# A decode kernel: the last weight matrix laid out in blocks of 14 and 13, a part of it in a transfer of 64 rows

## The chip, the cores and the metric

The kernel runs on one core of one Trainium2 chip. The metric is the device time of one execution, in microseconds; the kernel before has a median of 712.53 us over three runs (712.04 to 712.59). A core has the engines TensorE (PE in the profile, with its weight loads as PEld), VectorE (DVE), ScalarE (ACT), GpSimd (POOL) and SyncE (SP), and sixteen DMA engines that move data from the chip's memory into the on-chip store. SP does no arithmetic here: it only issues the loads.

## The reference

Two rounds of the same two layers on a batch of four tokens, with the same weights and the same caches in both rounds:

```python
x = A_x                                              # 4 x 1 x 640
for _ in range(2):
    x = x + A(layernorm(x), k_cache, v_cache, wq, wo)   # attention
    x = x + B(layernorm(x), w1, w2)                     # MLP

# A: 32 heads of 128, the last 1024 of 4096 cached keys
q = x @ wq ; s = einsum("bhqd,bhkd->bhqk", q, k) * 128 ** -0.5
o = einsum("bhqk,bhkd->bhqd", softmax(s), v) ; return o @ wo
# B: 640 -> 1728 -> 640
return maximum(x @ w1, 0) @ w2
```

All arrays are 32-bit floats. The weights and caches don't fit on the chip together, so nearly all of them are read twice, some 300 MB in all, for very little arithmetic per byte.

## The kernel before, in words

The 128 partitions (rows) of the on-chip store hold the data; `store` is one large tile of five slots and a first part, `ring` and `kept` are small ones. The host lays all of a head's data (wq, keys, values, wo) out as one record of 9472 columns on 128 partitions; heads go through the slots one after another. `rec` is the tensor of the records and `wm` that of w1 and w2.

*The order of the loads.* The Python code first builds a list, `items`, of all loads in their order. `pump()` issues from its front on SP whenever `done(...)` has freed the columns that the next load will overwrite; it never reorders. Loads share eight completion semaphores in turn, and a load waits until the one eight places ahead of it has landed. So SP runs ahead of the data by at most eight loads.

*The order on the engines.* `InOrder` (the helper in which nearly every instruction is recorded, so that most profile rows carry its line, L102) issues the instructions of each engine in the order in which the code calls them.

*Round two's MLP*, `mlp(1)`, stands at the end of the program. The transposed, normalised x is in `xT`; `h_ps` is a PSUM bank. For each of five blocks of w1, four matmuls write h for a quarter j of the 1728 features, 432 columns wide, on partitions 32j to 32j+3. VectorE then transposes h in blocks of 32 x 32 into `hT` (a view of `scratch`), and takes the maximum with zero times the layer norm's factor. So features lie in `hT` as block m of each quarter on 32 partitions: thirteen full blocks of 32 and one of 16, since 432 is 13 times 32 and 16 more. w2 is stored to match: `TILES` lists 52 pieces of 128 partitions x 160 columns (block m, output quarter n) and, as entries 28 and 29, two more that pack the half blocks of 16 features (`ENDS`); each of these two is used by two matmuls. The DVE copy of 16 columns ahead of the second transpose lets the two halves of those packed pieces meet the right features.

*Loads of w2 in round two.* They come last of all, in four loads of 22, 20, 8 and 4 pieces (`W2_SLOT`), into the slot that head 23's record had; w1 goes to the slot beside it, in three loads. The heads 24, 25 and 26 are the last three of the round. `query`, `scores`, `values` and `project` are what a head does on TensorE, in this order; `project`, with wo at the end of a record, is the last.

*Fillers.* `busy()` is a matmul of no use to the result, on 328 columns unless another width is given, into spare columns of `acc`. They stand where TensorE would wait. A matmul of 32-bit floats is recorded as two passes, each with a weight load, so a filler counts as two in the profile.

After the last w2 matmul VectorE copies `acc` to `x_sb` (in `scratch`) and SP stores it as `out`.

Of the kernel before, what the change touches and what calls it, by code (L numbers as in the profile page):

```python
# [38 lines left out]
P = 128  # L39
B, D, H, DH, W, FF = 4, 640, 32, 128, 1024, 1728  # L40
NB = 4
FD = D // NB
# [10 lines left out]
FQ = FF // NB  # L53

TILES = [(m, n) for m in range(13) for n in range(NB)]
ENDS = 28
TILES[ENDS:ENDS] = [(13, 0), (13, 1)]
TCOLS = len(TILES) * FD
RING = 4320
KEPT = WO - 4 * 512  # L60
FIRST = K + 3 * 512
# [2 lines left out]
W2 = KB * FF  # L64
WM = W2 + TCOLS


W2_RING = [8, 5, 16, 10, 11, 4]
# [6 lines left out]

CUTS = [*range(0, K, DH), *range(K, WO, 512), *range(WO, REC + 1, FD)]
W1_SLOT = [[0, 1], [2, 3], [4]]
W2_SLOT = [22, 20, 8, 4]
LATE = 6


# [25 lines left out]


@with_exitstack
def decode_kernel(ctx: ExitStack, tc: tile.TileContext, xf, rec, wm, out):  # L110
    nc = tc.nc
    pe, dve, act, pool, sp = (InOrder(tc, e) for e in (nc.tensor, nc.vector, nc.scalar, nc.gpsimd, nc.sync))
    sb = ctx.enter_context(tc.tile_pool(name="sb", bufs=1))
# [10 lines left out]
    hT = scratch.rearrange("p (m j) -> p m j", j=32)  # L124
# [4 lines left out]
    rows = sb.tile([P, 2 * B], F32, name="rows")  # L129
# [6 lines left out]
    store = sb.tile([P, FIRST + NS * REC], F32, name="store")  # L136
    kept = sb.tile([P, REC - KEPT], F32, name="kept")
    ring = sb.tile([P, RING], F32, name="ring")

# [3 lines left out]
    acc = ps.tile([P, 512], F32, name="acc")  # L143
# [30 lines left out]
    LAST = H - NS  # L174


    def home(h, r):

        if r:
            return FIRST + (h if h >= LAST else h - 6 + LAST) % NS * REC  # L180
        return (0 if h < NS else FIRST) + h % NS * REC

    items = []
# [3 lines left out]
    spare = home(H - 1, 0)  # L187
    buffers = {"store": store, "ring": ring, "kept": kept}

    def load(src, lo, hi, buf, col, parts):  # L190
        items.append((src[:, lo:hi], buf, col, hi - lo, parts))

    def place(buf, col):
        return ("store", spare + FROM + col) if buf == "spare" else (buf, col)

    def weight(r, lo, hi, buf, col):
        buf, col = place(buf, col)
        load(wm, lo, hi, buf, col, [(("w", r), lo, hi, col)])


    def run(r, lo, hi, buf, col):
        parts = [(("rec", r, h), max(lo - h * REC, 0), min(hi - h * REC, REC), col + max(h * REC - lo, 0))
                 for h in range(lo // REC, (hi - 1) // REC + 1)]
        load(rec, lo, hi, buf, col, parts)
# [44 lines left out]
    for lo, hi, buf, col in IN_RING:  # L249
# [3 lines left out]
        (0, V, 0, WO), (2, 0, 2, V), (1, V, 1, REC), (3, 0, 3, V), (2, V, 2, REC), (3, V, 4, FROM))]  # L253
    places += [("store", 0, FIRST), ("store", old[4] + FROM, old[4] + REC), ("ring", 0, RING)]
    cuts = [h * REC + x for h in new[1:6] for x in CUTS]
    c, end = new[1] * REC, new[6] * REC
    for buf, lo, hi in places:
        if lo == old[1]:
            piece(1, new[0], WO, REC, buf, lo)
        elif c < end:  # L260
            cut = max(x for x in cuts if x <= min(end, c + hi - lo))
            run(1, c, cut, buf, lo)
            c = cut
# [6 lines left out]
    ending(1, hs, False)  # L270
    for ks in W1_SLOT:
        weight(1, ks[0] * FF, (ks[-1] + 1) * FF, "store", home(LAST + 1, 0) + ks[0] * FF)
    n = 0
    for size in W2_SLOT:
        weight(1, W2 + n * FD, W2 + (n + size) * FD, "store", home(LAST + 2, 0) + n * FD)
        n += size

    def pump():

        while items:  # L280
            src, buf, col, n, parts = items[0]
            if any(b == buf and x < col + n and col < y for b, x, y in live):
                return
            sp.dma_start(buffers[buf][:, col:col + n], src)
            live.append((buf, col, col + n))
            for key, lo, hi, c in parts:
                at.setdefault(key, []).append((lo, hi, buf, c))
            items.pop(0)

    def pieces(key):  # L290
        return at[key if key in at else (key[0], 0) + key[2:]]

    def cols(key, lo, n):

        for x, y, buf, col in pieces(key):
            if x <= lo and lo + n <= y:
                return buffers[buf][:, col + lo - x:col + lo - x + n]
        raise KeyError((key, lo, n))

    def done(key, lo, hi):  # L300

        if key[0] == "rec" and key[1] == 0 and key[2] >= LAST:
            return
        if key == ("rec", 0, 0):
            lo = max(lo, FIRST)
# [36 lines left out]
    h_ps, warm = sc_ps[0][:, :512], sc_ps[0][:, 512:]  # L342
# [7 lines left out]
    def busy(n=328, to=spare_cols, groups=1):  # L350

        for g in range(groups):
            pe.matmul(to[32 * g:32 * g + 1, :n], ones, kept[:, :n], start=to is not spare_cols, stop=True,
                      skip_group_check=True)
# [17 lines left out]
    def deviation(bias, scale, by_row):  # L372

        var = variances.pop()
        pe.matmul(var, ones.to_broadcast([P, P]), squares, start=False, stop=True, skip_group_check=True)
        act.activation(rrow, var, AF.Sqrt, bias=bias, scale=scale / D)
        dve.reciprocal(rrow, rrow)
        if by_row:
            dve.tensor_tensor(mrt, rrow, of_batch, op=OP.mult)
            dve.tensor_reduce(rstd, mrt, op=OP.add, axis=AX.X)  # L380

    def xblock(k):
        return xT[:, 32 * k:32 * k + B]
# [77 lines left out]
    def mlp(r):  # L461


        for k in range(KB):
            for j in range(NB):
                pe.matmul(h_ps[32 * j:32 * j + B, :FQ], xblock(k), cols(("w", r), k * FF + FQ * j, FQ),
                          start=(k == 0), stop=(k == KB - 1))
                if not r and FF < k * FF + FQ * (j + 1) in [hi for _, hi, _, _ in MLP_RING]:
                    busy()
            done(("w", r), k * FF, k * FF + FF)  # L470
            if k == 0:
                deviation(eps, 1.0, False)
                busy(256, warm)
        busy()
        busy(256)
        for lo, hi in ((0, 224), (224, 480)):
            if lo:
                dve.tensor_copy(h_ps[:, 464:480], h_ps[:, 416:FQ])
            dve.transpose(scratch[:, lo:hi], h_ps[:, lo:hi])
            h = hT[:, lo // 32:hi // 32, :B]  # L480
            dve.scalar_tensor_tensor(h, h, 0.0, rrow.unsqueeze(1).to_broadcast([P, (hi - lo) // 32, B]),
                                     op0=OP.max, op1=OP.mult)
        key = ("w", r)
        sizes = W2_SLOT if r else W2_RING
        first = 0
        for i, size in enumerate(sizes):
            for s in range(first, first + size):
                m, n = TILES[s]
                w = cols(key, W2 + s * FD, FD)
                for part, q in ((m, n),) if m < 13 else ((13, n), (14, n + 2)):  # L490
                    pe.matmul(acc[32 * q:32 * q + B, :FD], hT[:, part, :B], w,
                              start=False, stop=(s >= len(TILES) - NB), skip_group_check=True)
            if r == 0 and i < len(sizes) - 2:
                busy()
            done(key, W2 + first * FD, W2 + (first + size) * FD)
            first += size


    pump()
    pe.matmul(acc[:, :FD], ident, x_sb, start=True, stop=False, skip_group_check=True)  # L500
    for r in range(2):
# [12 lines left out]
        for n, h in enumerate(hs[:-2]):  # L514
            i = n - (H - late)
            s = (n + 1) % 2
# [44 lines left out]
        for i in (late - 3, late - 1, late - 2) if late > 2 else (1,):  # L561
            project(r, hs[H - late + i], i, i == late - 2 or late == 2)
        center(256, 328)
        mlp(r)
    dve.tensor_copy(x_sb, acc[:, :FD])
    sp.dma_start(out, x_sb)
# [37 lines left out]
```

## Time and profile before

| | |
|---|---|
| median of three runs | 712.53 us (712.04 to 712.59) |
| the profiled execution | 712.55 us, of which 710.7 us are its span |
| moved from memory | 301.97 MB, mean 425 GB/s over the span |
| TensorE busy, mean granted clock | 502.4 us (71%), 0.824 |
| VectorE busy, ScalarE busy | 317.4 us (45%), 99.6 us (14%) |

The span is what the profile's clock counts; 1.85 us of the execution lie outside it. A busy share is an average over the whole span. The DMA share of a window is the mean busy share of the sixteen DMA engines in it. In a timeline a row begins with its start and its busy time in us; behind the shapes and the count, a bracket gives the idle time of the engine ahead of it and what ended that.

### The profile page before, as it was taken

What the parts mean: (1) busy time and instruction counts of PE and PEld (TensorE: products, weight loads), DVE (VectorE), ACT (ScalarE), POOL (GpSimd) and SP (SyncE); (2) the same over time, 40 slices, a digit from 0 to 9 for tenths busy, and PEclk for the clock granted to TensorE, in tenths of its full rate; (3) what the DMA queues carried; (4) which work ended last, traced back from release to release, by engine and by line L of the source; (5) the groups of instructions that cost most, each with busy time, mean ns of one, the idle gap of its engine ahead of it and who ended that gap; (6) DMA issues with size and microseconds to landing.
All of it is one profiled execution on the core that took longest, in us unless ns stands there. A gap on an engine that the chain in (4) does not pass through costs nothing.

```text
span 710.7 us, 8613 instructions
## 1 busy us (share of the span) xinstructions
PE 502.4 (71%) x3722; PEld 199.5 (28%) x3722; DVE 317.4 (45%) x645; ACT 99.6 (14%) x210; POOL 1.1 (0%) x9
## 2 busy tenths in 40 slices
PE   0675677576677686868788998756577685695985
PEld 0331322231332222333223333322222231332322
DVE  2252344253443353546541866625244253453661
ACT  0210111011010110111130421201010011011120
POOL 0000000000000000000000000000000000000000
PEclk9987787677676778788999999969687677788899
DMA  9999999999999999999999999999999999999996
GB/s 397 436 416 451 422 435 447 417 435 447 420 429 451 427 429 420 425 444 420 426 404 396 411 425 434 447 429 436 442 431 433 434 428 436 430 427 421 430 427 281
DMA packets 12741, 301.97 MB, mean 425 GB/s; under 512 B 1424, under 2 KB 1568, under 8 KB 4640
## 3 DMA queue, kind: packets, MB, share of 16 engines
q1 hardware_dynamic: 12672, 301.42, 98.9%
q8 instruction: 29, 0.48, 0.2%
q14 instruction: 8, 0.07, 0.0%
q10 hardware_dynamic: 32, 0.01, 0.0%
HBM read 301.34 MB, written 0.08 MB: 424 GB/s over the span
## 4 chain that ended last, share of the span: by engine, by line
DMA 68%; PE 25%; DVE 4%; another core or an unknown queue 1%; ACT 1%; issue 1%; SPq 0%; ACTq 0%
DMA store<-rec 60%; PE sc_ps L102 10%; PE o_ps L102 7%; DMA store<-wm 5%; PE acc L102 3%; PE misc L102 3%; DMA ring<-wm 3%; DVE scratch L102 2%; DVE o_ps L102 2%; PE t_ps L102 2%; ACT oTs L102 1%; DVE small L102 0%; ACT sc_ps L102 0%; DVE sc_ps L102 0%
## 5 line engine op out<-in xcount | busy, mean ns | idle before, releaser
L102 PE MATMUL sc_ps<-store,qT 128*4 128x512 f32 x1024 | 193.7, 852 | 37.8 <-DMA store<-rec 36.4
L102 PE MATMUL misc<-xT,store 128*128 128x4 f32 x620 | 92.8, 276 | 100.6 <-DMA store<-rec 100.0
L102 DVE TENSOR_REDUCE small<-sc_ps 128x1 f32<-128x1024 f32 x64 | 78.4, 1224 | 157.9 <-PE sc_ps L102 157.8
L102 PE MATMUL o_ps<-store,scratch 128*16 128x512 f32 x960 | 142.1, 667 | 4.6 <-DVE scratch L102 2.9
L102 PEld LDWEIGHTS misc<-xT,store 128*128 128x128 f32 x620 | 87.4, 221 | 156.2 <-DMA store<-rec 123.1
L102 ACT ACTIVATE sc_ps<-sc_ps,small 128x1024 f32<-128x1024 f32 x64 | 69.8, 1091 | 325.2 <-DVE small L102 325.2
L102 DVE STREAM_TRANSPOSE sc_ps<-sc_ps 128x1024 f32<-128x1024 f32 (+1 forms) x70 | 81.7, 1167 | 0.1
L102 PEld LDWEIGHTS sc_ps<-store,qT 128*4 128x4 f32 x1024 | 32.7, 107 | 121.2 <-issue 66.4
L102 PEld LDWEIGHTS o_ps<-store,scratch 128*16 128x16 f32 x960 | 32.3, 114 | 118.6 <-issue 100.7
L102 DVE TENSOR_TENSOR o_ps<-o_ps,of_block 128x512 f32<-128x512 f32 x62 | 43.4, 699 | 45.9 <-PE o_ps L102 45.8
L102 DVE TENSOR_TENSOR qT<-misc,rows 128x4 f32<-128x4 f32 x61 | 9.5, 156 | 112.7 <-PE misc L102 112.6
L102 PE MATMUL acc<-store,oTs 128*4 128x160 f32 x488 | 34.6, 365 | 17.1 <-ACT oTs L102 17.0
L102 DVE TENSOR_REDUCE scratch<-o_ps 128x128 f32<-128x512 f32 x62 | 42.9, 692 | 2.1
L102 ACT COPY oTs<-t_ps 128x4 f32<-128x4 f32 x59 | 9.6, 162 | 204.5 <-PE t_ps L102 204.5
L102 PE MATMUL t_ps<-rows,scratch 128*128 128x4 f32 x118 | 25.5, 286 | 11.4 <-DVE scratch L102 10.9
L102 PEld LDWEIGHTS t_ps<-rows,scratch 128*128 128x128 f32 x118 | 21.4, 226 | 17.9 <-DVE scratch L102 14.2
L102 DVE TENSOR_TENSOR scratch<-sc_ps,mrt 128x128 f32<-128x128 f32 (+1 forms) x70 | 19.6, 280 | 2.7
L102 PE MATMUL acc<-kept,small 128*1 128x328 f32 (+2 forms) x54 | 17.4, 428 | 0.0
L99 PE MATMUL acc<-scratch,ring 128*128 128x160 f32 x2 | 0.9, 540 | 22.2 <-DMA scratch<-xf 22.2
L102 DVE TENSOR_SCALAR mrt<-of_batch,small 128x4 f32<-128x4 f32 x64 | 14.7, 230 | 2.2
L102 DVE STREAM_TRANSPOSE scratch<-small 128x32 f32<-128x32 f32 x64 | 12.9, 202 | 2.4 <-ACT sc_ps L102 2.4
L102 PEld LDWEIGHTS acc<-store,oTs 128*4 128x4 f32 x488 | 6.9, 84 | 22.9 <-ACT oTs L102 21.9
(84 smaller groups left out, 123.1 us busy)
## 6 DMA issues: line engine op xcount, KB each, us to landing
store<-rec SPq DMA_DIRECT2D x14, 7872.0 KB, 28.9
store<-rec SPq DMA_DIRECT2D x7, 7936.0 KB, 30.9
store<-rec SPq DMA_DIRECT2D x4, 7104.0 KB
store<-rec SPq DMA_DIRECT2D x11, 2368.0 KB, 34.8
store<-rec SPq DMA_DIRECT2D x3, 4736.0 KB, 27.2
store<-rec SPq DMA_DIRECT2D x2, 4416.0 KB, 28.3
store<-rec SPq DMA_DIRECT2D x5, 1024.0 KB, 20.2
store<-rec SPq DMA_DIRECT2D x1, 4160.0 KB, 20.7
```

What stands on the lines that cost most here:

```text
L99: r = build(*args, **kwargs)
L102: r = build(*args, **kwargs)
```

## The change

In round two the 1728 features are no longer cut into four quarters of 432 but into 448, 448, 416 and 416: fourteen whole blocks of 32 on the first two, thirteen on the last two. The w2 pieces of the first thirteen blocks are then whole for all four parts (52 pieces, `EVEN`, a new tensor `w2`). What is left, block 13 of the first two parts, is 64 features: a tensor `halves`, loaded to partitions 0 to 63 by a transfer of its own of 64 rows x 640 columns, ahead of the other w2 loads. On the host `halves` is 8 rows, each with 8 x 640 numbers and 32 more of padding, so that the transfer's source is a pattern of 8 groups x 8 rows x 640. The loads of w2 become `halves` and 22, 18, 8 and 4 pieces. The total of w2's bytes is the same: 54 x 128 x 160 x 4 = 52 x 128 x 160 x 4 + 64 x 640 x 4 = 4,423,680. The DVE copy of 16 columns goes, the second transpose takes 224 columns in place of 256. The 256-column filler behind w1 takes 328 columns, one more filler stands behind it, and two behind the first w2 load's matmuls and those of `halves`. Round one is left as it was.

On SP, the end of the queue (`halves` and `w`, as the listing cuts the name w2, are the new tensors; DMAHW0 to 7 are the eight completion semaphores, and PE a wait for TensorE to be done with old contents). Before:

```order
L102 DMA store<-wm 128x1728 [waits DMAHW6_49,PE_49]
L102 DMA store<-wm 128x3520 [waits DMAHW7_49]
L102 DMA store<-wm 128x3200 [waits DMAHW0_49,PE_49]
L102 DMA store<-wm 128x1280 [waits DMAHW1_49,PE_49]
L102 DMA store<-wm 128x640 [waits DMAHW2_49,PE_49]
L102 DMA out<-scratch 128x160 [waits DMAHW3_49,DVE_49]
```

Now:

```order
L107 DMA store<-wm 128x1728 [waits DMAHW6_49,PE_49]
L107 DMA store<-halves 64x1x640 [waits DMAHW7_49,PE_49]
L107 DMA store<-w 128x3520 [waits DMAHW0_49]
L107 DMA store<-w 128x2880 [waits DMAHW1_49]
L107 DMA store<-w 128x1280 [waits DMAHW2_49]
L107 DMA store<-w 128x640 [waits DMAHW3_49]
L107 DMA out<-scratch 128x160 [waits DMAHW4_49,DVE_49]
```

One load more stands ahead of the four, each of these waits for the next semaphore in the turn, and all the waiting for TensorE is now at `halves`, whose columns (8320 to 8959 of the slot) reach into head 23's wo.

On PE, from the last matmuls with w1 to the end (`sc_ps` rows with xT are w1, `acc` rows with scratch are w2, `kept,small` the fillers). Before:

```order
L102 MATMUL sc_ps_73<-store,xT 4x432 [waits DMAHW6_49]
L102 MATMUL sc_ps_73<-store,xT 4x432 x3
L102 MATMUL acc<-kept,small 1x328 [waits Activation_49]
L102 MATMUL acc<-kept,small 1x256
L102 MATMUL acc<-store,scratch 4x160 [waits DMAHW7_49,DVE_49]
L102 MATMUL acc<-store,scratch 4x160 x21
L102 MATMUL acc<-store,scratch 4x160 [waits DMAHW0_49]
L102 MATMUL acc<-store,scratch 4x160 x5
L102 MATMUL acc<-store,scratch 4x160 [waits DVE_49]
L102 MATMUL acc<-store,scratch 4x160 x15
L102 MATMUL acc<-store,scratch 4x160 [waits DMAHW1_49]
L102 MATMUL acc<-store,scratch 4x160 x7
```

Now:

```order
L107 MATMUL acc<-kept,small 1x328 [waits Activation_49]
L107 MATMUL acc<-kept,small 1x328 x2
L107 MATMUL acc<-store,scratch 4x160 [waits DMAHW0_49,DVE_49]
L107 MATMUL acc<-store,scratch 4x160 x21
L107 MATMUL acc<-store,scratch 4x160 [waits DMAHW7_49,DVE_49]
L107 MATMUL acc<-store,scratch 4x160 x3
L107 MATMUL acc<-kept,small 1x328 x2
L107 MATMUL acc<-store,scratch 4x160 [waits DMAHW1_49]
L107 MATMUL acc<-store,scratch 4x160 x17
L107 MATMUL acc<-store,scratch 4x160 [waits DMAHW2_49]
L107 MATMUL acc<-store,scratch 4x160 x7
L107 MATMUL acc<-store,scratch 4x160 [waits DMAHW3_49]
```

The four matmuls with the left-over features move from the second w2 load to just behind the first, with two fillers behind them; the second load has 18 matmuls in place of 22, and the two last loads keep their 8 and 4.

The diff, cut to its core:

```diff
+WIDE = [14 * 32, 14 * 32, 13 * 32, 13 * 32]
+FROM_F = [0, WIDE[0], 2 * WIDE[0], 2 * WIDE[0] + WIDE[2]]
+EVEN = [(m, n) for m in range(13) for n in range(NB)]
+HALF_ROWS = P // 2
...
-W2_SLOT = [22, 20, 8, 4]
+W2_SLOT = [22, 18, 8, 4]
...
+    c = home(LAST + 2, 0)
+    load(halves[:, :8 * D].rearrange("g (p c) -> g p c", c=D), 0, D, "store", c + len(EVEN) * FD,
+         [(("halves",), 0, D, c + len(EVEN) * FD)], HALF_ROWS)
     n = 0
     for size in W2_SLOT:
-        weight(1, W2 + n * FD, W2 + (n + size) * FD, "store", home(LAST + 2, 0) + n * FD)
+        load(w2, n * FD, (n + size) * FD, "store", c + n * FD, [(("w2",), n * FD, (n + size) * FD, c + n * FD)])
         n += size
...
-            sp.dma_start(buffers[buf][:, col:col + n], src)
+            sp.dma_start(buffers[buf][:rows, col:col + n], src)
...
-                pe.matmul(h_ps[32 * j:32 * j + B, :FQ], xblock(k), cols(("w", r), k * FF + FQ * j, FQ),
+                lo, n = (FROM_F[j], WIDE[j]) if r else (FQ * j, FQ)
+                pe.matmul(h_ps[32 * j:32 * j + B, :n], xblock(k), cols(("w", r), k * FF + lo, n),
                           start=(k == 0), stop=(k == KB - 1))
...
-        busy(256)
-        for lo, hi in ((0, 224), (224, 480)):
-            if lo:
+        busy(328 if r else 256)
+        if r:
+            busy()
+        for lo, hi in ((0, 224), (224, 448 if r else 480)):
+            if lo and not r:
                 dve.tensor_copy(h_ps[:, 464:480], h_ps[:, 416:FQ])
...
+            if r and i == 0:
+                for q in range(NB):
+                    pe.matmul(acc[32 * q:32 * q + B, :FD], hT[:HALF_ROWS, 13, :B],
+                              cols(("halves",), q * FD, FD)[:HALF_ROWS], start=False, stop=False, skip_group_check=True)
+            if i < (1 if r else len(sizes) - 2):
                 busy()
-            done(key, W2 + first * FD, W2 + (first + size) * FD)
+                if r:
+                    busy()
+            done(key, base + first * FD, base + (first + size) * FD)
...
+    quads = [w2[lo:lo + n].reshape(-1, 32, D) for lo, n in zip(FROM_F, WIDE)]
+    even = [np.concatenate([f[m] for f in quads])[:, FD * n:FD * n + FD] for m, n in EVEN]
+    halves = np.concatenate([f[13] for f in quads[:2]]).reshape(8, 8 * D)
...
+        "w2": np.concatenate(even, 1),
+        "halves": np.pad(halves, ((0, 0), (0, 32))),
```

More of the change, by code (lines that the diff above doesn't have):

```diff
@@ L109, in decode_kernel @@
 @with_exitstack
-def decode_kernel(ctx: ExitStack, tc: tile.TileContext, xf, rec, wm, out):
+def decode_kernel(ctx: ExitStack, tc: tile.TileContext, xf, rec, wm, w2, halves, out):
     nc = tc.nc
@@ L188, in decode_kernel, with load @@
     buffers = {"store": store, "ring": ring, "kept": kept}
-    def load(src, lo, hi, buf, col, parts):
-        items.append((src[:, lo:hi], buf, col, hi - lo, parts))
+    def load(src, lo, hi, buf, col, parts, rows=P):
+        items.append((src[:, lo:hi] if rows == P else src, buf, col, hi - lo, parts, rows))
     def place(buf, col):
@@ L280, in pump @@
         while items:
-            src, buf, col, n, parts = items[0]
+            src, buf, col, n, parts, rows = items[0]
             if any(b == buf and x < col + n and col < y for b, x, y in live):
                 return
-            sp.dma_start(buffers[buf][:, col:col + n], src)
+            sp.dma_start(buffers[buf][:rows, col:col + n], src)
             live.append((buf, col, col + n))
@@ L482, in mlp @@
                                      op0=OP.max, op1=OP.mult)
-        key = ("w", r)
-        sizes = W2_SLOT if r else W2_RING
+        if r:
+            key, base, sizes, tiles = ("w2",), 0, W2_SLOT, EVEN
+        else:
+            key, base, sizes, tiles = ("w", r), W2, W2_RING, TILES
         first = 0
@@ L487, in mlp @@
             for s in range(first, first + size):
-                m, n = TILES[s]
-                w = cols(key, W2 + s * FD, FD)
+                m, n = tiles[s]
+                w = cols(key, base + s * FD, FD)
                 for part, q in ((m, n),) if m < 13 else ((13, n), (14, n + 2)):
                     pe.matmul(acc[32 * q:32 * q + B, :FD], hT[:, part, :B], w,
-                              start=False, stop=(s >= len(TILES) - NB), skip_group_check=True)
-            if r == 0 and i < len(sizes) - 2:
+                              start=False, stop=(s >= len(tiles) - NB), skip_group_check=True)
+            if r and i == 0:
[3 more added lines that the diff above has]
+            if i < (1 if r else len(sizes) - 2):
                 busy()
-            done(key, W2 + first * FD, W2 + (first + size) * FD)
+                if r:
+                    busy()
+            done(key, base + first * FD, base + (first + size) * FD)
             first += size
```

## The prediction

> **What bounds the kernel.** I read the page's head first, then the chain of waits at its end, then the last microseconds in windows.
>
> ```profile
> span 710.7 us, 8613 instructions
> DMA  9999999999999999999999999999999999999996
> DMA packets 12741, 301.97 MB, mean 425 GB/s; under 512 B 1424, under 2 KB 1568, under 8 KB 4640
> q1 hardware_dynamic: 12672, 301.42, 98.9%
> q8 instruction: 29, 0.48, 0.2%
> q10 hardware_dynamic: 32, 0.01, 0.0%
> scratch<-xf ACTq DMA_DIRECT2D x4, 2.5 KB
> ```
>
> All sixteen DMA engines are busy in every slice but the last. At 425 GB/s over sixteen, one engine moves 26.6 GB/s, that is 26.6 KB in a microsecond. Only what changes the bytes of the engine that ends last, or what comes behind it, can move the time. The chain of waits, from its end:
>
> ```profile
> 672.66 32.17 DMA store<-wm
> 704.83 0.04 issue
> 704.87 2.79 PE acc L102 x68
> 707.66 0.02 issue
> 707.68 0.32 DVE scratch L102
> ```
>
> The second w2 load lands at 704.83, TensorE works through the rest, VectorE copies, and the store of `out` ends the span at 710.7. But the chain names the load that TensorE waited longest for, not the last one. The weight loads of TensorE show both waits:
>
> ```profile
> 697.51 0.08 PEld L102 LDWEIGHTS acc<-kept,small 128*1 128x1 f32 x1 [0.28 <-issue]
> 697.87 0.08 PEld L102 LDWEIGHTS acc<-kept,small 128*1 128x1 f32 x1 [0.28 <-issue]
> 698.42 0.08 PEld L102 LDWEIGHTS acc<-kept,small 128*1 128x1 f32 x1 [0.19 <-issue]
> 701.15 1.49 PEld L102 LDWEIGHTS acc<-store,scratch 128*4 128x4 f32 x44 [2.64 <-issue]
> 704.87 2.00 PEld L102 LDWEIGHTS acc<-store,scratch 128*4 128x4 f32 x60 [2.24 <-DMA store<-wm]
> 707.16 0.11 PEld L102 LDWEIGHTS acc<-store,scratch 128*4 128x4 f32 x8 [0.29 <-DMA store<-wm]
> ```
>
> TensorE starts the first w2 load's 22 matmuls (44 passes) at 701.15, the second's at 704.87, and at 706.87 it has done all but the last four matmuls; it waits 0.29 us and starts them at 707.16, when the last load has landed. So the last load sets the end, with 0.29 us to spare ahead of TensorE's own work. The windows show how that last load comes in (in each row: PE, PEld, DVE, ACT, POOL busy, then the granted clock, the DMA share and GB/s):
>
> ```profile
> 701.50:702.00 0.50, 0.50 (x22) 0.40 (x17) 0.00 (x0) 0.00 (x0) 0.00 (x0) 1.00 0.92 389
> 702.00:702.50 0.50, 0.50 (x24) 0.42 (x14) 0.00 (x0) 0.00 (x0) 0.00 (x0) 1.00 0.98 410
> 702.50:703.00 0.50, 0.48 (x12) 0.10 (x2) 0.00 (x0) 0.00 (x0) 0.00 (x0) 1.00 0.91 379
> 703.00:703.50 0.50, 0.00 (x0) 0.00 (x0) 0.00 (x0) 0.00 (x0) 0.00 (x0) 1.00 0.74 307
> 703.50:704.00 0.50, 0.00 (x0) 0.00 (x0) 0.00 (x0) 0.00 (x0) 0.00 (x0) 1.00 0.64 261
> 704.00:704.50 0.50, 0.00 (x0) 0.00 (x0) 0.00 (x0) 0.00 (x0) 0.00 (x0) 1.00 0.54 220
> 704.50:705.00 0.50, 0.13 (x4) 0.11 (x8) 0.00 (x0) 0.00 (x0) 0.00 (x0) 1.00 0.39 159
> 705.00:705.50 0.50, 0.50 (x20) 0.40 (x16) 0.00 (x0) 0.00 (x0) 0.00 (x0) 1.00 0.42 169
> 705.50:706.00 0.50, 0.50 (x24) 0.39 (x20) 0.00 (x0) 0.00 (x0) 0.00 (x0) 1.00 0.42 140
> 706.00:706.50 0.50, 0.50 (x19) 0.35 (x14) 0.00 (x0) 0.00 (x0) 0.00 (x0) 1.00 0.17 67
> 706.50:707.00 0.50, 0.50 (x20) 0.34 (x10) 0.00 (x0) 0.00 (x0) 0.00 (x0) 1.00 0.04 15
> ```
>
> The share falls from 0.98 to 0.04 over four microseconds: the sixteen engines do not end together. Summed from 702.0 the shares make 5.25 half-slices, 2.63 us; engines that ended together would be done at 704.6, while the last one ends near 706.8 (0.04 of sixteen engines over half a microsecond is one engine for 0.3 us). At 704.5 about half of the engines, 0.54 to 0.39 of sixteen, still work. So there are an early half and a late half, and the end belongs to the late one. Why they differ no view says; the 29 instruction packets of 0.48 MB (16.5 KB each, 0.6 us of one engine at the rate above) are a likely reason, if they do not fall on all engines alike.
>
> **The change, part by part.**
>
> *The w2 bytes per engine.* Loads of 128 rows make up queue q1, 12,672 packets: 88 loads of 144, that is 128 rows and 16 closing packets, one for each engine, so eight rows an engine. The second load's rows are shortened from 20 to 18 pieces, 2 x 160 x 4 = 1,280 bytes a row: every engine loses 8 x 1,280 = 10,240 bytes, 0.385 us. What comes back is `halves`, 64 rows of 2,560 bytes. No load of the trace has 64 rows. The nearest are the four loads of xf, of four rows each: 32 packets on q10, eight a load, four rows and four closing ones, so four engines. Over sixteen engines, `halves` gives each four rows, 10,240 bytes: net nothing. On eight, it gives each 20,480 bytes: net +0.385 us on those eight and -0.385 us on the others. These are the two ends of the price at the engine that ends last, -0.385 and +0.385 us, with 0 between them. The source is written as eight groups, and xf's rows show a small pattern confined to as many engines as it has rows, so eight engines are nearer than sixteen. Of the two eights, I take the early half for partitions 0 to 63, since a load that runs from partition 0 and can't fill sixteen engines most plausibly begins at the first; that the first are the early ones rests on the half-and-half shape above alone, and is the weakest step. The early half, done by about 704.7, then ends by about 705.1, still ahead of the late half's 706.4. Sum of this part: -0.385 us.
>
> [...]
>
> *Start of the w2 loads.* SP's queue:
>
> ```profile
> 663.66 3.67 SPq L102 DMA_DIRECT2D store<-wm  x2
> 672.66 0.33 SPq L102 DMA_DIRECT2D store<-wm  x1
> 678.24 0.33 SPq L102 DMA_DIRECT2D store<-wm  x1
> 683.87 0.33 SPq L102 DMA_DIRECT2D store<-wm  x1
> ```
>
> and, of TensorE's timeline, head 23's `project`:
>
> ```profile
> 673.28 0.46 PE L102 MATMUL acc<-store,oTs 128*4 128x160 f32 x8 [0.31 <-ACT oTs L102]
> ```
>
> Before, the four w2 loads are issued at 667.0, 672.66, 678.24 and 683.87, each when its semaphore's last load has landed. `halves` waits for head 23's wo, which this row frees at 673.74; the first w2 load behind it then goes out at about 674.4 in place of 667.0, the others one semaphore further on, the last by 689.5 (683.87 and one more spacing of 5.6 us). TensorE's last matmuls with w1 end only with the filler's weight load at 697.51, so w1's data fill the DMA engines until shortly before that, and even the latest has some 7 us in hand. One issue more is 0.33 us on SP. Cost 0; if the cover were gone, each microsecond late would be a microsecond.
>
> *TensorE.* w1 keeps 20 matmuls, with the same 1,728 columns a block. Behind it stand six filler passes in place of four: at 0.28 us from one to the next (697.87 to 698.42 in two steps) they reach to 699.3, and the first w2 load lands at 701.1. The four matmuls of `halves` move ahead: after 702.64 eight passes at 0.033 us (2.00 us for 60) to 702.9, then two fillers, four passes of 0.28, to 704.0. The second load is due at 704.83 - 0.385 = 704.45. So 0.4 us in hand. Its 36 passes take 1.2 us in place of 44 in 1.5. Then 8 and 4 matmuls as before, so the 0.29 us of waiting ahead of the last four stays, or grows. Cost 0, gain 0: the last load still sets the end. A `halves` load that came late would hold all w2 matmuls behind it; it stands ahead of the first of them in the queue.
>
> *VectorE.*
>
> ```profile
> 698.12 0.42 DVE L102 STREAM_TRANSPOSE scratch<-sc_ps 128x224 f32<-128x224 f32 x1 [3.00 <-PE sc_ps L102]
> 698.68 0.18 DVE L102 COPY sc_ps<-sc_ps 128x16 f32<-128x16 f32 x1
> 698.89 0.45 DVE L102 STREAM_TRANSPOSE scratch<-sc_ps 128x256 f32<-128x256 f32 x1
> 699.37 0.19 DVE L102 SCALAR_TENSOR_TENSOR scratch<-scratch,rows 128x32 f32<-128x32 f32 x1
> ```
>
> The copy goes (0.18 us) and the second transpose shrinks from 0.45 to 0.42: `hT` is whole at 699.35 instead of 699.56. Its user starts at 701.15, so it gains nothing.
>
> **Sum.** 712.55 - 0.385 = 712.17 in the profiled execution's time; the median stands 0.02 lower, so 712.15 us.
>
> **Rivals.**
>
> *Sixteen engines share `halves`.* Net 0: 712.5. For it: all of q1's loads do so. Against it: the source's eight groups.
>
> *Eight engines, and the late ones among them.* The last load lands at 707.5 in place of 707.12: 712.9. For it: nothing in the rows tells which half is late.
>
> *The clock falls at the end (slower).* The windows show a granted clock of 1.00 up to the end, though in the span's mean it is 0.824. With the clock at one half from 701 on, passes double: 44 take 3.0 us to 704.1, eight more 0.5, four filler passes 2.2, to 706.9, and the 60 left 4.0, to 710.9 in place of 707.3: about 716. It decides once TensorE's work behind the first load is over 0.7 us longer, the 0.4 us ahead of the second load and the 0.29 us of waiting behind it. [...]
>
> *Faster by more than the shift.* Were the last engines relieved by more than their 10,240 bytes, up to 706.8 - 704.6 = 2.2 us would be there to win; nothing in the change moves that much.
>
> **Chances and range.** Early half: 0.50, 712.15. Sixteen engines: 0.20, 712.5. Late half: 0.17, 712.9. The clock, or SP's wait or another cause above 714: 0.08. A gain that I don't see: 0.05. The runs before scatter over 0.55 us, and 0.2% (1.43 us) is about what a measurement of this kernel can tell from no change; the first three cases lie within it. So faster 0.05, same 0.87, slower 0.08. The range takes the three cases with that scatter at both ends: 711.5 to 713.4.
>
> **What would show it.** In the windows behind 702, the DMA share should stay higher up to 705 and end about 0.4 us earlier; TensorE's last weight loads should start at about 706.8 with an idle time from a DMA ahead of them, and the second load's at 704.5. If the share falls as before and the last weight loads start at 707.2, sixteen engines had `halves`; at 707.5, the wrong eight. Issues of w2 behind 690 on SP, or a clock under 1.00 behind 700, would make it wrong.

## The result, and the profile after

The changed kernel takes 713.47 us (median of 18 runs, 712.72 to 715.07) beside 712.22 us for the kernel before (18 runs, 710.77 to 713.78): 1.25 us slower by the medians, a ratio of 1.0019 with a 95% interval of 1.0012 to 1.0026. The forecast was 712.15 us, 0.38 us faster; the measured time lies just above its range.

Head and queues of the page of the changed kernel:

```profile
span 711.7 us, 8624 instructions
DMA packets 12813, 301.97 MB, mean 424 GB/s; under 512 B 1432, under 2 KB 1576, under 8 KB 4712
q1 hardware_dynamic: 12744, 301.42, 98.9%
```

The bytes are the same. Queue q1 has 72 packets more: 64 rows and eight closing packets. So `halves` is on eight engines, as forecast. SP's timeline and the end of the chain of waits of the changed kernel:

```profile
672.61 0.76 SPq L107 DMA_DIRECT2D store<-halves  x1
673.43 0.40 SPq L107 DMA_DIRECT2D store<-w  x1
685.66 0.33 SPq L107 DMA_DIRECT2D store<-w  x1
```

```profile
673.43 28.16 DMA store<-w
701.60 0.14 issue
701.73 6.96 PE acc L107 x112
708.69 0.02 issue
708.72 0.33 DVE scratch L107
```

The issues are early enough, as forecast. But the chain now enters TensorE at the first w2 load, landed at 701.60, and from there on TensorE never waits: it sets the end, at 708.69 in place of 707.66. Its weight loads and, below, the windows (columns as in the prediction) say why:

```profile
701.70 2.65 PEld L107 LDWEIGHTS acc<-store,scratch 128*4 128x4 f32 x44 [2.84 <-issue]
704.88 0.11 PEld L107 LDWEIGHTS acc<-store,scratch 64*4 64x4 f32 x8 [0.54 <-issue]
706.57 1.72 PEld L107 LDWEIGHTS acc<-store,scratch 128*4 128x4 f32 x49 [0.19 <-issue]
```

```profile
701.00:702.00 1.00, 0.27 (x8) 0.25 (x12) 0.00 (x0) 0.00 (x0) 0.00 (x0) 0.96 0.94 398
703.00:704.00 1.00, 1.00 (x24) 0.64 (x17) 0.00 (x0) 0.00 (x0) 0.00 (x0) 0.50 0.83 347
706.00:707.00 1.00, 1.00 (x25) 0.52 (x24) 0.00 (x0) 0.00 (x0) 0.00 (x0) 1.00 0.14 54
707.00:708.00 1.00, 1.00 (x39) 0.72 (x32) 0.00 (x0) 0.00 (x0) 0.00 (x0) 1.00 0.00 0
```

In this execution the clock was 0.50 around 703, so the weight loads of the first 44 passes took 2.65 us in place of 1.49, and the two fillers and the rest came behind the data: no byte of a load moves after 707. That is the slower rival of the prediction, at a third of its price (TensorE ends 1.0 us later, not 3.6), for by 706 the clock was back at 1.00. It is also a trap: it is one execution, and the experiments show that the cost of the change is mostly another one. That one stands in windows that the chain passes by, ahead of 699. First the kernel before, then the changed one:

```profile
693.00:695.00 2.00, 2.00 (x21) 0.72 (x23) 0.57 (x4) 0.26 (x1) 0.00 (x0) 1.00 1.00 422
695.00:697.00 2.00, 2.00 (x28) 0.62 (x24) 0.12 (x1) 0.00 (x0) 0.00 (x0) 1.00 1.04 445
```

```profile
693.00:695.00 2.00, 2.00 (x24) 0.92 (x27) 0.18 (x1) 0.27 (x1) 0.00 (x0) 1.00 1.03 327
695.00:697.00 2.00, 1.36 (x17) 0.25 (x11) 0.00 (x0) 0.00 (x0) 0.00 (x0) 1.00 1.09 346
```

The DMA engines are as busy as before, but move 327 and 346 GB/s in place of 422 and 445. Over these four microseconds that is (422 + 445 - 327 - 346) x 2 us = 388 KB fewer, 0.9 us of the kernel's mean rate of 425 GB/s.

The trace also holds a time for every DMA packet (one row of a load is one packet), and the packets show the same without an average. In the kernel before, all 128 packets of the first w2 load, 14,080 bytes each, take 526 ns; in the changed kernel 72 of the 128 take over 540 ns, up to 907. At 694.5 us sixteen packets are in flight, as many as there are engines, and all are slow (those of 14,080 bytes 671 to 834 ns, those of 6,912 bytes 367 to 491 in place of 262), though only one of them is of `halves`: the engines that carry nothing of it at that moment lose as well. From 670 us on, the packets of q1 take 19.4 us more in all than the usual times of their sizes, 1.2 us for each of the sixteen engines; in the kernel before it is 0.06 us.

### The profile page after: what moved, and what is told of

It is laid out like the page before. It is cut to its first block, busy times and chain, and to the rows that moved or that the text cites. A ratio compares the mean times of both kernels' runs of the same rounds, so it can differ in the third digit from the quotient of the medians.

```text
span 711.7 us, 8624 instructions
## 1 busy us (share of the span) xinstructions
PE 507.8 (71%) x3728; PEld 200.7 (28%) x3728; DVE 317.4 (45%) x644; ACT 99.8 (14%) x210; POOL 1.1 (0%) x9
## 4 chain that ended last, share of the span: by engine, by line
DMA 69%; PE 24%; DVE 4%; another core or an unknown queue 1%; ACT 1%; issue 1%; SPq 0%; ACTq 0%
DMA store<-rec 62%; PE sc_ps L107 9%; PE o_ps L107 7%; DMA store<-w 4%; PE acc L107 4%; DMA ring<-wm 3%; PE misc L107 3%; DVE scratch L107 2%; DVE o_ps L107 2%; PE t_ps L107 1%; ACT oTs L107 1%; DVE small L107 0%; ACT sc_ps L107 0%; SPq L107 0%
## 5 line engine op out<-in xcount | busy, mean ns | idle before, releaser
L107 PE MATMUL o_ps<-store,scratch 128*16 128x512 f32 x960 | 144.8, 681 | 2.6 <-DMA store<-rec 1.9
L107 PE MATMUL acc<-kept,small 128*1 128x328 f32 (+2 forms) x60 | 19.3, 431 | 0.0
```

The costliest lines, as they stand in the source:

```text
L107: r = build(*args, **kwargs)
```

## The experiments

All ran beside runs of the kernel before on the same chip. "Layout" stands for the 14 and 13 blocks with the 64-row transfer. The diffs are cut (... marks what is left out); where an expectation says "with the fillers of the kernel before", the lines that put these back, shown with the first run, are left out too.

**Fillers or transfer.** The first four take the parts of the change asunder.

> The new layout of w2 and the 64-row transfer stay, the fillers are those of the kernel before. Two theories for the 1.25 us that the change costs. Theory F: it is TensorE, which behind the first w2 load has two fillers on its path and which, where the granted clock has fallen to one half there, is still at work when the last load has landed. Theory H: it is the 64-row transfer, whose eight DMA engines include some that end last. F: with the fillers gone about 0.2 us slower than before (712.4 beside 712.2), the last passes again started by a landing. H: all of the cost stays, 1.0 us or more slower.

```diff
-        busy(328 if r else 256)
-        if r:
-            busy()
+        busy(256)
...
-            if i < (1 if r else len(sizes) - 2):
+            if r == 0 and i < len(sizes) - 2:
                 busy()
-                if r:
-                    busy()
```

> The kernel before with the three changed or added fillers of round two alone (328 columns in place of 256, one more behind w1, two behind the first w2 load). F: 0.7 to 1.1 us slower than before, and in a profile in which the clock is one half around 702 TensorE ends its work about 1 us behind the last landing. H: no difference within 0.2 us.

```diff
-        busy(256)
+        busy(328 if r else 256)
+        if r:
+            busy()
...
-            if r == 0 and i < len(sizes) - 2:
+            if i < (1 if r else len(sizes) - 2):
                 busy()
+                if r:
+                    busy()
```

> The changed kernel, but the 64-row transfer's source is 64 rows and not 8 groups of 8, so that sixteen engines can share it. F: the same as the changed kernel within 0.3 us, 0.8 to 1.3 us slower than before. H: within 0.3 us of before.

```diff
-    load(halves[:, :8 * D].rearrange("g (p c) -> g p c", c=D), 0, D, "store", c + len(EVEN) * FD,
+    load(halves[:, :D], 0, D, "store", c + len(EVEN) * FD,
...
-    halves = np.concatenate([f[13] for f in quads[:2]]).reshape(8, 8 * D)
+    halves = np.concatenate([f[13] for f in quads[:2]])
```

> The changed kernel without the two fillers behind the first w2 load; the wider and the added filler behind w1 stay. F: most of the cost goes, 0.1 to 0.4 us slower than before, as in the run without any new filler. H: no change against the changed kernel, 1.0 us or more slower than before.

```diff
-            if i < (1 if r else len(sizes) - 2):
+            if r == 0 and i < len(sizes) - 2:
                 busy()
-                if r:
-                    busy()
```

Measured, as ratios to the kernel before with 95% intervals: the layout alone 1.0014 (1.0005 to 1.0023), the fillers alone 1.0005 (0.9996 to 1.0014), sixteen engines 1.0022 (1.0011 to 1.0033), the change without the two fillers 1.0007 (0.9998 to 1.0015). So the layout costs without any new filler, and the fillers cost nothing that can be told from zero without the layout: theory F, that TensorE is the cause, fails on the first run (it allowed 0.2 us, and the interval begins at 0.4); the second, whose interval reaches 1.0 us, speaks against F but does not exclude it. Theory H, that it is the bytes on eight engines, fails on the third: on sixteen engines (12,752 packets on q1, 80 more than before) the cost is no smaller, though each then has the same bytes as before. Its windows have the low rate too:

```profile
693.00:695.00 2.00, 1.97 (x14) 0.58 (x12) 1.07 (x5) 0.68 (x1) 0.00 (x0) 1.00 1.04 339
695.00:697.00 2.00, 2.00 (x24) 1.09 (x27) 0.18 (x1) 0.26 (x1) 0.00 (x0) 1.00 1.06 329
```

The fourth run came out as F had it and not H: 0.09 us slower by the medians, where H wanted 1.0 us or more. But its interval holds F's 0.1 to 0.4 us as well as 1.0 us, and its profile has the low rate like the others (315 and 311 GB/s in the same windows), so its time decides nothing.

**The clock.** What was left of F was a guess, theory C: that TensorE's idle stretch ahead of the first w2 load, longer with the layout (2.84 us in the profile of the changed kernel, 2.64 in that of the kernel before), drops the clock.

> The changed kernel with five fillers of 328 columns behind w1 (in place of three) and none behind the first w2 load, so that TensorE idles some 1.2 us ahead of that load in place of 2.2 to 3. Theory C: the clock. [...] Theory T: the transfer of 64 rows makes the last load late, whatever TensorE does. C: within 0.3 us of before, with no executions 1.5 us above the median. T: as slow as the layout with the old fillers, 0.9 us above before.

Against the run without the two fillers behind the first w2 load:

```diff
         if r:
-            busy()
+            for _ in range(3):
+                busy()
```

> The same fillers with the 64-row transfer over sixteen engines. C: the 1.6 us that this transfer cost with the fillers of the changed kernel go; within 0.3 us of the run with five fillers and eight engines, and of before. T: still 1 us or more slower than before.

The edit is that of the run before, on the kernel with sixteen engines.

> The kernel before with five fillers of 328 columns behind round two's w1 in place of 328 and 256, nothing else. C: never slower, 0 to 0.4 us faster, since some executions of the kernel before have the clock at one half as well. T: no difference.

```diff
-        busy(256)
+        busy(328 if r else 256)
+        if r:
+            for _ in range(3):
+                busy()
```

> The kernel before without its two fillers behind round two's w1: the idle stretch ahead of the first w2 load grows from 2.4 to 3.6 us. C: the clock falls in nearly every execution, TensorE's work on w2 takes twice as long and ends behind the last landing: 1.0 to 2.0 us slower, and the profile shows a clock of 0.5 around 702. T: no difference.

```diff
-        busy()
-        busy(256)
+        if not r:
+            busy()
+            busy(256)
```

Measured: 1.0014 (1.0006 to 1.0023), 1.0014 (1.0005 to 1.0022), 1.0009 (0.9992 to 1.0027) and 1.0003 (0.9982 to 1.0023). With the idle stretch filled the layout costs as much as without; and the kernel before, robbed of both fillers, is no slower (median 712.05 beside 712.35). That last interval is too wide to exclude the 1.0 us that C wanted, but the profile has a clock of 1.00 from 700 to the end of TensorE's work, where C wanted 0.5. So theory C falls on both. That some executions of the kernel before have the clock at one half there is not shown either: its profile has 1.00 from 690 to 709. What the runs with the layout have in common is another thing, in the windows of all of them; here those of the layout alone:

```profile
693.00:695.00 2.00, 1.85 (x18) 0.85 (x22) 1.16 (x6) 1.35 (x2) 0.00 (x0) 1.00 1.03 359
695.00:697.00 2.00, 2.00 (x24) 0.77 (x19) 0.24 (x2) 0.26 (x1) 0.00 (x0) 1.00 1.05 351
```

**Where the slow stretch comes from.** Its clock is 1.00, and it lies where the engines are in `halves`, one after another: in the changed kernel the packets of `halves` run from 691.62 to 696.79 us, and slow packets from about 692.3 to 697.8. Not each of them slows the rest: the packets that run beside the first ones, up to about 692.2, take their usual time, but for one next to a packet of instructions (13,824 bytes in 1,028 ns in place of 516).

> In every run with the new layout, fillers or not, eight engines or sixteen, the DMA share stays at 1.0 from 693 to 697 us but the rate falls from some 430 GB/s to 310 to 360, and only there. This kernel is the one before in all but one thing: round two's w2, in the old pieces, comes from a tensor of its own. Theory N: engines that read the tensor w2 beside others that still read w1 in wm slow each other. Theory S: the 64-row load of the small tensor slows all engines as long as some are in it. N: under 370 GB/s from 693 to 697, and 0.7 to 1.2 us slower than before. S: above 405 GB/s there, and within 0.3 us of before.

```diff
...
-        weight(1, W2 + n * FD, W2 + (n + size) * FD, "store", home(LAST + 2, 0) + n * FD)
+        c = home(LAST + 2, 0) + n * FD
+        load(w2, n * FD, (n + size) * FD, "store", c, [(("w", 1), W2 + n * FD, W2 + (n + size) * FD, c)])
...
+        "w2": np.concatenate(tiles, 1),
```

> The new layout with the 64-row load and the fillers of the kernel before, but round two's w1 and the 52 w2 pieces stand in one tensor, as in the kernel before. N: above 405 GB/s from 693 to 697, and at most 0.4 us slower than before (the 20 KB more on the engines that share the 64-row load). S: under 370 GB/s there and some 0.9 us slower.

```diff
-        weight(1, ks[0] * FF, (ks[-1] + 1) * FF, "store", home(LAST + 1, 0) + ks[0] * FF)
+        lo, hi = ks[0] * FF, (ks[-1] + 1) * FF
+        load(w2, lo, hi, "store", home(LAST + 1, 0) + lo, [(("w", 1), lo, hi, home(LAST + 1, 0) + lo)])
...
-        load(w2, n * FD, (n + size) * FD, "store", c + n * FD, [(("w2",), n * FD, (n + size) * FD, c + n * FD)])
+        load(w2, W2 + n * FD, W2 + (n + size) * FD, "store", c + n * FD, [(("w2",), n * FD, (n + size) * FD, c + n * FD)])
...
-        "w2": np.concatenate(even, 1),
+        "w2": np.concatenate([block_rows(np.asarray(B_w1)).transpose(1, 0, 2).reshape(P, KB * FF), *even], 1),
```

> The new layout with the fillers of the kernel before; the small load moves the same bytes as 128 rows of 320 columns and not 64 of 640, so each of sixteen engines has eight rows in it. The four matmuls of the left-over features then read other numbers than they should; their work is the same. N: the slow stretch stays, under 370 GB/s, 0.7 us or more slower than before. S, if it is the 64 rows: above 405 GB/s and within 0.3 us of before; S, if it is any small load there: as N.

```diff
-    load(halves[:, :8 * D].rearrange("g (p c) -> g p c", c=D), 0, D, "store", c + len(EVEN) * FD,
-         [(("halves",), 0, D, c + len(EVEN) * FD)], HALF_ROWS)
+    load(halves, 0, D // 2, "store", c + len(EVEN) * FD, [(("halves",), 0, D // 2, c + len(EVEN) * FD)])
...
-                              cols(("halves",), q * FD, FD)[:HALF_ROWS], start=False, stop=False, skip_group_check=True)
+                              cols(("halves",), q % 2 * FD, FD)[:HALF_ROWS], start=False, stop=False, skip_group_check=True)
...
-    halves = np.concatenate([f[13] for f in quads[:2]]).reshape(8, 8 * D)
+    halves = np.concatenate([f[13] for f in quads[:2]]).reshape(P, D // 2)
```

> The new layout with the fillers of the kernel before; the 64-row load goes ahead of w1 into the free end of w1's slot, so that it comes some 10 us earlier, among the last loads of head data. N: the slow stretch stays at 693 to 697, and the cost with it. S: the slow stretch moves to about 683 to 687, the windows from 693 to 697 show above 405 GB/s, and the cost of 0.9 us stays, since the bytes behind it come later all the same.

```diff
+    early = home(LAST + 1, 0) + KB * FF
+    load(halves[:, :8 * D].rearrange("g (p c) -> g p c", c=D), 0, D, "store", early, [(("halves",), 0, D, early)], HALF_ROWS)
     for ks in W1_SLOT:
...
-    load(halves[:, :8 * D].rearrange("g (p c) -> g p c", c=D), 0, D, "store", c + len(EVEN) * FD,
-         [(("halves",), 0, D, c + len(EVEN) * FD)], HALF_ROWS)
```

In this order, the windows of the old pieces from a tensor of their own:

```profile
693.00:695.00 2.00, 1.96 (x22) 0.73 (x14) 1.13 (x5) 1.07 (x1) 0.00 (x0) 1.00 1.03 434
695.00:697.00 2.00, 2.00 (x24) 0.83 (x23) 0.18 (x1) 0.26 (x1) 0.00 (x0) 1.00 1.04 444
```

of the layout with w1 and w2 in one tensor:

```profile
693.00:695.00 2.00, 1.71 (x16) 0.89 (x16) 0.77 (x4) 1.45 (x2) 0.00 (x0) 1.00 1.03 379
695.00:697.00 2.00, 2.00 (x21) 0.76 (x23) 0.55 (x4) 0.26 (x1) 0.00 (x0) 1.00 1.01 363
697.00:699.00 2.00, 2.00 (x30) 0.84 (x24) 0.08 (x1) 0.00 (x0) 0.00 (x0) 1.00 1.02 357
```

of 128 rows of 320:

```profile
693.00:695.00 2.00, 1.71 (x15) 0.84 (x16) 0.81 (x4) 1.45 (x2) 0.00 (x0) 1.00 1.06 435
695.00:697.00 2.00, 2.00 (x21) 0.79 (x23) 0.54 (x4) 0.26 (x1) 0.00 (x0) 1.00 1.05 443
```

and of the 64 rows ahead of w1:

```profile
681.00:683.00 2.00, 1.74 (x19) 0.57 (x19) 1.52 (x6) 0.00 (x0) 0.00 (x0) 1.00 1.00 356
683.00:685.00 2.00, 1.69 (x26) 0.64 (x18) 1.45 (x3) 0.35 (x2) 0.00 (x0) 1.00 1.03 313
693.00:695.00 2.00, 1.96 (x14) 0.58 (x12) 1.07 (x5) 0.67 (x1) 0.00 (x0) 1.00 1.05 438
```

The stretch follows the 64-row load wherever it stands, whatever tensors the others read, and the same bytes in 128 rows make none. Theory N is out. Two things came out less neatly than S had them: the first window of the layout in one tensor, 379 GB/s, is above the 370 that S set, and the stretch of the 64 rows ahead of w1 stands at 681 to 685 and not 683 to 687. And the times do not say it by themselves. The ratios are 0.9989 (0.9971 to 1.0008), 0.9999 (0.9989 to 1.0010), 0.9999 (0.9989 to 1.0009) and 1.0007 (0.9997 to 1.0018); single executions of the kernel before reached 719.5 us beside these runs, and the layout in one tensor does not show by this ratio the 0.9 us that S wanted of it.

**What in the 64 rows.** The last three deal the same rows out to the engines in other ways, on the author's guess that the dealing is what slows all engines; theory R, in the first of them, is the other guess.

> The new layout with the fillers of the kernel before; the 64 rows come as two loads of 32 rows, each with a source of 8 groups of 4 rows, so that it is confined to eight engines with four neighbouring rows each. [...] Theory R: any load of fewer than 128 rows slows the others. [...]

```diff
-    load(halves[:, :8 * D].rearrange("g (p c) -> g p c", c=D), 0, D, "store", c + len(EVEN) * FD,
-         [(("halves",), 0, D, c + len(EVEN) * FD)], HALF_ROWS)
+    srcs = [halves[8 * g:8 * g + 8, :4 * D].rearrange("g (p c) -> g p c", c=D) for g in range(2)]
+    load(srcs, 0, D, "store", c + len(EVEN) * FD, [(("halves",), 0, D, c + len(EVEN) * FD)], 32)
...
-            sp.dma_start(buffers[buf][:rows, col:col + n], src)
+            for g, one in enumerate(src if rows == 32 else [src]):
+                sp.dma_start(buffers[buf][rows * g:rows * g + rows, col:col + n], one)
...
-    halves = np.concatenate([f[13] for f in quads[:2]]).reshape(8, 8 * D)
+    halves = np.concatenate([f[13] for f in quads[:2]]).reshape(16, 4 * D)
```

> The same two loads of 32 rows, to the same places, with the same bytes, but with 32 plain rows as source, so that sixteen engines have two rows each. [...] R: as in the run with groups of four, slow in both. [...]

Against the run before:

```diff
-    srcs = [halves[8 * g:8 * g + 8, :4 * D].rearrange("g (p c) -> g p c", c=D) for g in range(2)]
+    srcs = [halves[32 * g:32 * g + 32, :D] for g in range(2)]
...
-    halves = np.concatenate([f[13] for f in quads[:2]]).reshape(16, 4 * D)
+    halves = np.concatenate([f[13] for f in quads[:2]])
```

> The changed kernel with its own fillers and the two loads of 32 rows in groups of four. [...] If the fillers behind the first w2 load cost on their own in the new layout, it stays 0.4 us or more behind the same loads with the fillers of before.

The two loads of the first of these three, in the changed kernel with its own fillers. The windows of the three, and q1 of the first two, in the same order:

```profile
q1 hardware_dynamic: 12752, 301.42, 98.7%
...
693.00:695.00 2.00, 2.00 (x20) 0.69 (x19) 0.55 (x3) 0.26 (x1) 0.00 (x0) 1.00 1.02 430
695.00:697.00 2.00, 2.00 (x28) 0.97 (x24) 0.18 (x1) 0.00 (x0) 0.00 (x0) 1.00 1.03 439
```

```profile
q1 hardware_dynamic: 12768, 301.42, 99.0%
...
693.00:695.00 2.00, 1.97 (x22) 0.70 (x14) 1.12 (x5) 1.04 (x1) 0.00 (x0) 1.00 1.08 361
695.00:697.00 2.00, 2.00 (x24) 0.87 (x23) 0.18 (x1) 0.26 (x1) 0.00 (x0) 1.00 1.03 339
```

```profile
693.00:695.00 2.00, 2.00 (x18) 0.77 (x21) 0.55 (x3) 0.22 (x2) 0.00 (x0) 1.00 0.99 417
695.00:697.00 2.00, 2.00 (x27) 0.89 (x23) 0.18 (x1) 0.17 (x1) 0.00 (x0) 1.00 1.09 465
```

The packets show eight engines a load in the first (2 x 40 more than before) and sixteen in the second (2 x 48). Same rows, same bytes, same place in the queue: in fours on eight engines there is no slow stretch, in twos on sixteen there is. The packets say it more sharply: in the first all 128 of the first w2 load take 526 ns, in the second 65 of the 128 take over 540, up to 894. So it is not a load of few rows as such (R falls, at 430 and 439 GB/s) but how its rows are dealt to the engines. Why the dealing counts is not shown: no view tells which engine writes which partitions, in these loads or in the full ones. The ratios are 0.9990 (0.9969 to 1.0012), 1.0006 (0.9987 to 1.0025) and 0.9993 (0.9974 to 1.0011), the medians 712.32, 713.26 and 712.26 beside 712.33. The last is the whole change with only the transfer cut in two: it shows no cost any more, and is not measurably faster than the kernel before.

How the loss reaches the engines that carry nothing of the load stays open: in the changed kernel the packets of all sixteen slow down, those of the eight without a row of `halves` by 0.98 to 1.64 us an engine.

**All runs together.** Difference of the medians to the kernel before, measured beside it, in us:

| 64 or 32 rows, slow stretch in the profile | | no slow stretch | |
|---|---|---|---|
| the change | +1.25 | fillers alone | +0.21 |
| layout alone | +0.55 | five fillers, old layout | -0.10 |
| sixteen engines | +2.07 | no fillers, old layout | -0.30 |
| without the two fillers | +0.09 | own tensor | -0.04 |
| five fillers | +1.00 | 128 rows | -0.06 |
| sixteen engines, five fillers | +1.04 | two loads in fours | -0.01 |
| one tensor | +0.40 | two loads in fours, new fillers | -0.07 |
| 64 rows first | +0.92 | | |
| two loads in twos | +0.93 | | |

The means are +0.92 and -0.05 us; 0.9 us is what the rate in the windows gave. Single rows scatter, and four on the left (+0.09, +0.40, +0.92 and +0.93) have ratios whose intervals hold no change. The packets part the two columns without overlap: from 670 us on they take 0.95 to 1.31 us per engine more than usual in the nine kernels on the left, and 0.06 us in the seven on the right and in the kernel before. (This holds for the five fillers on the old layout too, whose profiled execution of 719.74 us lost its time before that.)

## Why the prediction was wrong, point by point

*Bytes per engine: the step that failed.* The price of `halves` was worked out as bytes on the engines that carry it, between -0.385 and +0.385 us, "with 0 between them". The number of engines, eight, was right (72 packets more). What was missing, put at nothing without a reason, is what such a load does to the engines that don't carry it: all sixteen together move a fifth to a quarter less while it is in flight (327 and 346 GB/s in place of 422 and 445), 0.9 us by the windows and 1.2 us per engine by the packets. Both ends of the price were too low, and the rows bound them badly: the nearest load, of xf, is four rows at the start of the kernel and shows nothing of a neighbour. That the load takes as long as five microseconds for 160 KB comes from the staggered engines which the prediction did see: each reaches `halves` in its own time.

*The early half.* That the eight engines are the early ones was called the weakest step. In the profiled execution it was wrong. The last packet of `halves` ends at 696.79, and the engine that has it still has eight rows of each w2 load ahead, 8 x (526 + 432 + 196 + 102) ns = 10.0 us: it ends at about 706.8, and the last packet of all ends at 706.9. So the engine that ends last is one of the eight, and for its bytes the other end of the price held, +0.385 us. Strung together by their times (each packet starts some 3 ns before the one ahead of it on its engine ends), the packets fall into sixteen rows; the eight with `halves` end at 703.5, 703.6, 704.1, 704.4, 705.3, 705.3, 706.6 and 706.9, early and late ones alike. In the kernel before, the ends spread from 702.8 to 706.8 in the same way: the falling share was read rightly as engines that end one after another, but not as two halves of which one is fixed. In the two loads in fours with the new fillers the last engine, at 706.4, has none of the 64 rows. Whether the moved bytes gain anything on average stays open: with the stretch gone, two runs stand at 0.9990 and 0.9993, with intervals that hold both the gain of 0.385 us (0.9995) and none.

*Start of the loads, VectorE.* Right. `halves` went out at 672.61 and the last w2 load at 685.66, ahead of need; VectorE's copy is gone and gains nothing.

*TensorE, cost 0.* Nothing measured speaks against it while the clock is at 1.00: the fillers alone 1.0005, and with the mended transfer 0.9993. In the profile of the latter (two loads in fours, new fillers) TensorE waits for each of w2's last three loads, so the last load sets the end as forecast:

```profile
704.41 1.18 PEld L107 LDWEIGHTS acc<-store,scratch 128*4 128x4 f32 x36 [0.58 <-DMA store<-w]
705.93 0.38 PEld L107 LDWEIGHTS acc<-store,scratch 128*4 128x4 f32 x16 [0.34 <-DMA store<-w]
706.72 0.11 PEld L107 LDWEIGHTS acc<-store,scratch 128*4 128x4 f32 x8 [0.40 <-DMA store<-w]
```

In the profiled execution of the changed kernel the clock was at one half from 702 to past 705 (0.50 in the windows of 1 us up to 705, 0.83 in the next), and TensorE set the end. The prediction had this as its slower rival; its condition, TensorE's work behind the first load more than 0.7 us longer, was met: the weight loads of the first 44 passes alone took 1.16 us more, and the first load had landed half a microsecond later (701.60). The profile of the two loads in fours with the fillers of before shows it too, a window with the clock at 0.50 and weight loads

```profile
705.00:707.00 2.00, 1.94 (x32) 1.11 (x36) 0.00 (x0) 0.00 (x0) 0.00 (x0) 0.50 0.18 72
705.06 3.83 PEld L107 LDWEIGHTS acc<-store,scratch 128*4 128x4 f32 x60 [1.10 <-DMA store<-w]
```

that take 3.83 us; that execution took 714.16 us. So it happens now and then, with and without the new fillers: in two of the seventeen profiles. Whether the two fillers make it dearer where the slow stretch is there too is not settled: with them stand +1.25 and +2.07 us, without them +0.09 to +1.04.

*Rivals and the range.* Sixteen engines would have been no better: measured, +2.07 us. The late half, at 712.9, had the bytes of the engine that ends last right in the profiled execution, and still none of what was missing. The range took the scatter of three runs (0.55 us) for that of the kernel; eighteen runs reach over 3.0 us.

## What to carry to other kernels

A transfer's cost is not only its own bytes: look at GB/s beside the DMA share, and where the share stays at 1.0 while the rate falls (here 1.03 with 327 GB/s in place of 1.00 with 422), look for the odd-shaped load in flight. As a first try, deal a load of fewer than 128 rows out to the engines in another way; here two loads of 32 rows in eight groups of four cost nothing that could be measured (ratios 0.9990 and 0.9993), and one of 64 rows cost about 0.9 us. Where single times scatter more than the effect, the times of single packets can still tell. And where the chain of waits of one execution shows a cause, take that cause away before believing it: here the clock was on the chain and the transfer was not.

## What was not expected of the hardware

160 KB to partitions 0 to 63, in one load of 64 rows or in two of 32 dealt in twos to sixteen engines, lowered the rate of all sixteen engines together from some 430 GB/s to between 311 and 379 for four to five microseconds, in the profiles of all nine kernels with such loads, and in none of the eight others, the kernel before among them. Engines that carry nothing of the load lose nearly as much: in the changed kernel seven of those eight lose 0.98 to 1.04 us each, and the eighth, with a packet of instructions between, 1.64; the eight that carry it lose 1.06 to 1.46. So here a transfer to one half of the partitions slowed what ran beside it.
